# Linear attention block: the inverse deviation of the first four tiles computed on GpSimd, and one weight load moved ahead of one load of x

## The chip, the cores and the metric

The kernel runs on one core of a Trainium2 chip. Its time is the device time in microseconds (us) of one execution. Median before: 105.94 us over 3 runs (105.9 to 106.11).

A core has five engines that run their own instruction streams in order and meet through semaphores: TensorE (PE in the profile; its weight loads are PEld), VectorE (DVE), ScalarE (ACT), GpSimd (POOL) and SyncE (SP), which here only issues DMAs.

## The reference

Input x has 2048 rows of 640 columns, bf16. Three things are added up.

```python
x  = A_x
xn = (x - mean(x)) / sqrt(var(x) + 1e-5)          # per row
# A: linear attention with 32 heads of 20 columns
q, k, v = xn @ wqkv                                # 640 x 1920
phi(t) = where(t > 0, t + 1, exp(t)) + 1e-6
kv  = sum over rows of phi(k)^T v;  z = sum over rows of phi(k)
A   = (phi(q) kv / (phi(q) z + 1e-6)) @ wo
# B: the 8 rows with the largest x . w_r get a gated MLP, scaled by sigmoid(x . w_r)
out = x + A + (xn + MLP on its 8 rows)
```

B is applied to xn, so its row scores are xn times w_r, and its residual is xn. What the change touches is the first line: the mean and the inverse deviation of each row.

## The kernel before

The rows are worked in 16 tiles of 128 (`t` is the tile). Four stages follow each other: k for all tiles and the sum G = xn^T phi(k); q for all tiles; the small products of kv, wo and the MLP; and the output tiles. The change lies at the start of the first stage, in the code written out by hand for tiles 0 to 3. There is no scheduler: `ctx.enter_context(tc.manual_schedule())` is set, so each engine executes its instructions in the order in which the code issues them.

For one tile, the steps and their names are these.

- `ld(sp, XX[:, t, 1, :], ...)` (L103): SyncE issues the load of x. The loads of tiles 0 to 3, the second half of the k weights and the remaining tiles stand one after the other in SyncE's queue. The first half of the k weights goes through ScalarE's queue.
- `ln_a`, `ln_b` (L149, L152): VectorE takes the statistics of columns 0 to 319 and 320 to 639.
- `ln_g` (L155): VectorE makes mean and variance of them, in `MVf` (the aggregate).
- `ln_r` (L158, L159): ScalarE computes the inverse deviation `SR` as exp(-0.5 ln(var + eps)), two instructions on one column.
- `ln_xn` (L163): VectorE makes (x - mean) times SR. This is the normalization that the prediction speaks of. For tile 0 it comes in two parts, columns 0 to 255 and 256 to 639.
- `tr_mm` (L172): TensorE transposes the normalized tile into PSUM; `tr_cp` (L179 on ScalarE, L181 on VectorE) copies it to `xnT`.
- `K(t, (h,), ...)` (L208): TensorE multiplies with half h of the k weights, `wkh[h]`.
- `PHe`, `PHr`, `PHb` (L224, L227, L243): ScalarE takes exp and relu, VectorE combines them into `pk`, that is phi(k). `G` (L252, L259) sums over the rows.
- `ones(t)` (L265): GpSimd writes a column of ones into the normalized tile, for z.

From tile 4 on, the transposes are DMAs (L184) and the loop over t issues everything; `pool_extra` holds the building of constants that GpSimd does in the loop. `consts_e` and `bm2_copies` build a mask, `bm2`, that is first read where kv is masked, after the q stage.

Of the hand-written start, the part that matters reads as follows:

```python
    ln_a(0); ln_b(0); ln_a(1); ln_g(0); ln_b(1)
    ln_r(0)
    ln_g(1)
    ln_xn(0, ((0, 2 * P),))
    ln_r(1)
    ln_xn(0, ((2 * P, D),))
    ...
    ln_xn(1)
```

(The first line is five lines in the code.)

Of the kernel before, what the change touches and what calls it, by code (L numbers as in the profile page):

```python
# [7 lines left out]
P = 128  # L8
S = 2048
D = 640  # L10
# [13 lines left out]
EPS_BF16 = 1.0013580322265625e-05  # L24
# [6 lines left out]
F32 = mybir.dt.float32  # L31
# [3 lines left out]
ALU = mybir.AluOpType  # L35
# [3 lines left out]
def kernel(  # L39
# [13 lines left out]
    pe, dve, act, pool, sp = nc.tensor, nc.vector, nc.scalar, nc.gpsimd, nc.sync  # L53
# [3 lines left out]
    wqkv_v = A_wqkv.rearrange("(kc p) n -> p kc n", p=P)  # L57
# [9 lines left out]
    def st(shape, dt, name, tag=None):  # L67
        return sb.tile(shape, dt, name=name, tag=tag or name)
# [18 lines left out]
    lowkey = st([P, T], I32, "lowkey")  # L87
    eps6 = st([P, 1], F32, "eps6")
    eps5 = st([P, 1], F32, "eps5")
    lnv = st([P, T], F32, "lnv")  # L90
    rbf = st([P, T], BF16, "rbf")
    MVf = st([P, T, 2], F32, "MVf")
    MV = MVf[:].bitcast(BF16).rearrange("p t (k o) -> p t k o", o=2)[:, :, :, 1]
    SR = st([P, T], F32, "SR")
# [3 lines left out]
    HW = 320  # L98
    wkh = [wk[:, :, 0:HW], wk[:, :, HW + 64 :]]


    def ld(eng, dst, src):
        eng.dma_start(dst, src)  # L103
# [7 lines left out]
    ld(act, wkh[0], wqkv_v[:, :, D : D + HW])  # L111
    ld(sp, XX[:, 1, 1, :], x_v[:, 1, :])
    ld(sp, XX[:, 2, 1, :], x_v[:, 2, :])
    ld(sp, XX[:, 3, 1, :], x_v[:, 3, :])
    ld(sp, wkh[1][:, :, 0:HW], wqkv_v[:, :, D + HW : 2 * D])
    for a, b in ((4, 8), (8, 12), (12, 16)):
        ld(sp, XX[:, a:b, 1, :], x_v[:, a:b, :])
    sp.dma_start_transpose(xnT[:, 0:4, S - P : S], zero[:])
# [1 line left out]
    def warm4(w):  # L120
        pe.matmul(PS[:, 7, 0:w], lhsT=nc.const_aps.tensor(0.0, (P, P), F32),
                  rhs=nc.const_aps.tensor(0.0, (P, w), F32), start=True, stop=True)

    dve.memset(eps5[:], EPS_BF16)
    pool.memset(ident[:], 0.0)
    pool.affine_select(
        out=ident[:], in_=ident[:], compare_op=ALU.not_equal, fill=1.0,
# [19 lines left out]
    def ln_a(t):  # L147
        sts[t] = tmp.tile([P, 2, nc.vector.BN_STATS_DIM], F32, tag="stats", name="stats", bufs=4)
        dve.bn_stats(out=sts[t][:, 0, :], in_=XX[:, t, 1, 0:320])  # L149

    def ln_b(t):
        dve.bn_stats(out=sts[t][:, 1, :], in_=XX[:, t, 1, 320:D])  # L152

    def ln_g(t):
        dve.bn_aggr(out=MV[:, t, :], in_=sts[t][:])  # L155

    def ln_r(t):
        act.activation(lnv[:, t : t + 1], MV[:, t, 1:2], AF.Ln, bias=eps5[:])  # L158
        act.activation(SR[:, t : t + 1], lnv[:, t : t + 1], AF.Exp, scale=-0.5)  # L159

    def ln_xn(t, parts=((0, D),)):
        for a, b in parts:
            dve.tensor_scalar(out=XX[:, t, 0, a:b], in0=XX[:, t, 1, a:b], scalar1=MVf[:, t, 0:1],  # L163
                              scalar2=SR[:, t : t + 1], op0=ALU.subtract, op1=ALU.mult)
# [3 lines left out]
    def tr_mm(t, h, b0):  # L168
        k0, k1 = TRP[h]
        pt = PS[:, b0 + h, :].bitcast(BF16)  # L170
        for kc in range(k0, k1):
            pe.transpose(pt[:, (kc - k0) * P : (kc - k0 + 1) * P], XX[:, t, 0, kc * P : (kc + 1) * P], ident[:])  # L172

    def tr_cp(t, h, b0, eng):
        k0, k1 = TRP[h]
        src = PS[:, b0 + h, :].bitcast(BF16)[:, 0 : (k1 - k0) * P].rearrange("p (k c) -> p k c", c=P)
        dst = xnT[:, k0:k1, t * P : (t + 1) * P]
        if eng is act:
            act.copy(dst, src)  # L179
        else:  # L180
            dve.tensor_copy(dst, src)  # L181
# [17 lines left out]
    def off(t, h):  # L199
        return T - 1 - t if t != 1 and h else 0  # L200

    def K(t, hs=(0, 1), b=6, ks=range(KC)):
        for h in hs:
            if t > 4:
                pad(1)
            w = HW + h
            for kc in ks:
                pe.matmul(  # L208
                    PS[:, b + h, off(t, h) : off(t, h) + w],
                    lhsT=xnT[:, kc, t * P : (t + 1) * P],  # L210
                    rhs=wkh[h][:, kc, 0:w],
                    start=(kc == 0),
                    stop=(kc == KC - 1),
                )
# [6 lines left out]
    def PHe(t, h, b=6):  # L221
        if t not in phis:
            phis[t] = tuple(tmp.tile([P, D], BF16, tag=k, name=k, bufs=3) for k in ("ek", "rk"))
        act.activation(phis[t][0][:, h * HW : (h + 1) * HW], phi_src(t, h, b), AF.Exp)  # L224

    def PHr(t, h, b=6):
        act.activation(phis[t][1][:, h * HW : (h + 1) * HW], phi_src(t, h, b), AF.Relu)  # L227
# [17 lines left out]
    def pad(n):  # L245
        for _ in range(n):
            pe.ldweights(zero[:, 0:P])  # L247
# [30 lines left out]
    def band(ap, base, n, w=DH):  # L278
        for k, (b0, sg) in enumerate(((base, 1), (w - 1 - base, -1))):
            pool.affine_select(  # L280
                out=ap, in_=ap, compare_op=ALU.is_ge, fill=0.0,
                base=b0, pattern=[[-sg * w, n], [0, w]], channel_multiplier=sg,
            )

    def consts_e():
        pool.memset(bm2[0:E2, :], 1.0)
        band(bm2[0:E2, :], P, 8)

    def bm2_copies(gs):
        for g in gs:  # L290
            pool.tensor_copy(bm2[32 * g : 32 * g + 32, :], bm2[0:E2, :])
# [14 lines left out]
    def consts_d():  # L306
        pool.iota(lowkey[:], pattern=[[P, T]], base=P - 1, channel_multiplier=-1)

    pool_extra = {3: consts_b, 4: consts_c, 5: consts_d}

    wo_v = A_wo.rearrange("(g r) d -> r g d", r=GC)
    wg_v = B_w_gate.rearrange("(kc p) n -> p kc n", p=P)
# [19 lines left out]
                ld(sp, wg[:, k, :], wg_v[:, k, :])  # L332


    consts_e()
    bm2_copies((1, 2, 3))
    KA, KB = (range(0, 2), range(2, KC))
    ln_a(0)
    ln_b(0)
    ln_a(1)  # L340
    ln_g(0)
    ln_b(1)
    ln_r(0)
    ln_g(1)
    ln_xn(0, ((0, 2 * P),))
    ln_r(1)
    ln_xn(0, ((2 * P, D),))
    tr_mm(0, 0, 0)
    ln_xn(1)
# [5 lines left out]
    tr_cp(0, 1, 0, act)  # L355
    K(0, (0,), 6, KA)
    ln_b(2)
    tr_cp(1, 0, 2, act)
    tr_mm(1, 1, 2)
    ones(1)  # L360
    K(0, (0,), 6, KB)
    tr_cp(1, 1, 2, act)
    ln_g(2)
    ln_a(3)
    K(1, (0,), 4, KA)
    ln_r(2)
    ln_b(3)
    K(1, (0,), 4, KB)
    PHe(0, 0, 6)
    ln_xn(2)  # L370
    K(0, (1,), 6, KA)
    PHr(0, 0, 6)
    K(1, (1,), 4, KA)
    ln_g(3)
    ln_r(3)
    tr_mm(2, 0, 0)
    K(0, (1,), 6, KB)
    tr_cp(2, 0, 0, act)
# [113 lines left out]
    for t in range(T - 1):  # L492
# [13 lines left out]
                      op0=ALU.arith_shift_right, op1=ALU.bitwise_and)  # L506
# [445 lines left out]
```

## Time and profile before

| | us |
|---|---|
| median of 3 runs | 105.94 |
| the profiled execution | 105.91 |
| its span | 104.2 |
| TensorE busy | 99.8 (96%) |
| VectorE busy | 82.7 (79%) |
| ScalarE busy | 69.1 (66%) |
| GpSimd busy | 17.1 (16%) |

All times in the text are us from the start of the span. A row of the timeline or of the groups names the line, the engine, the operation, what it writes and reads with shapes, and how many. In the timeline the first number is the start and the second the length; a bracket at the end gives the idle time of the engine ahead of it and what ended it. Instructions of one engine overlap: the next one can start while the last one drains, so the distance between two starts is shorter than a length. In a DMA row the last number is the time from the issue to the landing. The granted TensorE clock was 1.00 in every stretch of the first 20 us of this run.

### The profile page before, as it was taken

To read this page: it belongs to the slowest core of one execution; us is meant where nothing else is said; L and a number is where in the kernel's file an instruction comes from. 1 tells how busy PE (TensorE), PEld (TensorE's weight loads), DVE (VectorE), ACT (ScalarE), POOL (GpSimd) and SP (SyncE) were. 2 spreads that over 40 slices of the span, in tenths; PEclk is the share of its full clock that TensorE was granted. 3 is DMA by queue.
4 is the path that set the end of the run, shared out by engine and by line. 5 is a ranking of instruction groups with operands and counts; after the bars stand their busy time and mean duration, and the time that the engine had idled before them with its cause. 6 is when DMAs were issued, how large, how long until landed. Compare 5 with 4: busy or idle time off the path is not lost.

```text
span 104.2 us, 2816 instructions
## 1 busy us (share of the span) xinstructions
PE 99.8 (96%) x944; PEld 72.5 (70%) x1176; DVE 82.7 (79%) x186; ACT 69.1 (66%) x174; POOL 17.1 (16%) x57
## 2 busy tenths in 40 slices
PE   6999999999999999999999999999999999999980
PEld 3347666668888888888877777875577667777760
DVE  1797999988888898873887886778988997888870
ACT  4289957666666666888599989997983997000000
POOL 7700000620000000000000064460001500000500
PEclk9999999999999999999999999999999999999999
DMA  2999937334557755889999999901760039983344
GB/s 63 298 307 377 325 66 69 66 66 92 135 127 92 140 124 124 191 248 359 224 399 249 360 406 382 319 22 31 217 236 9 12 110 270 280 289 122 126 129 126
DMA packets 23408, 19.77 MB, mean 190 GB/s; under 512 B 10978, under 2 KB 21858, under 8 KB 23394
## 3 DMA queue, kind: packets, MB, share of 16 engines
q1 hardware_dynamic: 22152, 19.11, 63.2%
q10 hardware_dynamic: 954, 0.46, 1.7%
q8 instruction: 8, 0.13, 0.6%
q0 software_dynamic: 288, 0.01, 0.3%
q14 instruction: 6, 0.05, 0.2%
HBM read 13.80 MB, written 3.65 MB: 168 GB/s over the span
## 4 chain that ended last, share of the span: by engine, by line
PE 89%; DVE 3%; DMA 2%; issue 2%; DVEq 0%
PE PS L208 21%; PE PS L480 21%; PE PS L751 20%; PE PS L252 16%; PE PS L259 4%; DMA XX<-in_A_x_dram 2%; PE PS L708 2%; PE PS L672 1%; PE PS L551 1%; PE PS L172 1%; PE PS L727 1%; PE PS L273 1%; DVE stats L149 1%; DVE XX L163 1%; DVE stats L152 1%
## 5 line engine op out<-in xcount | busy, mean ns | idle before, releaser
L208 PE MATMUL PS<-wk,xnT 128*128 128x320 bf16 (+1 forms) x160 | 25.2, 300 | 0.0
L252 PE MATMUL PS<-pk,XX 128*128 128x512 bf16 x75 | 22.7, 379 | 0.0
L247 PEld LDWEIGHTS <-zero 128*128 128x128 bf16 x224 | 18.2, 97 | 5.7
L480 PE MATMUL PS<-xnT,wq 128*128 128x512 bf16 x97 | 21.8, 379 | 0.3 <-issue 0.2
L751 PE MATMUL PS<-Mb,pqT 128*128 128x320 bf16 (+4 forms) x165 | 22.1, 295 | 0.0
L224 ACT ACTIVATE ek<-PS 128x320 bf16<-128x320 f32 x32 | 14.1, 441 | 9.9 <-PE PS L208 9.9
L751 PEld LDWEIGHTS <-pqT 128*128 128x128 bf16 x165 | 15.8, 98 | 4.5 <-issue 0.2
L208 PEld LDWEIGHTS <-xnT 128*128 128x128 bf16 x160 | 15.1, 97 | 4.5 <-ACT xnT L179 0.2
L243 DVE SCALAR_TENSOR_TENSOR pk<-ek,rk 128x640 bf16<-128x640 bf16 x16 | 13.1, 820 | 4.8 <-ACT rk L227 4.5
L542 DVE SCALAR_TENSOR_TENSOR pqT<-qe,qr 128x512 bf16<-128x512 bf16 x20 | 13.5, 682 | 2.5 <-ACT qr L489 2.5
L488 ACT ACTIVATE qe<-PS 128x512 bf16<-128x512 f32 x20 | 12.5, 624 | 2.9 <-PE PS L480 2.3
L259 PE MATMUL PS<-pk,XX 128*128 128x128 bf16 x64 | 14.0, 219 | 0.3
L227 ACT ACTIVATE rk<-PS 128x320 bf16<-128x320 f32 x32 | 14.0, 437 | 0.0
L480 PEld LDWEIGHTS <-wq 128*128 128x128 bf16 x100 | 11.6, 118 | 2.9
L489 ACT ACTIVATE qr<-PS 128x512 bf16<-128x512 f32 x20 | 12.5, 626 | 0.0
L760 DVE TENSOR_TENSOR o<-PS,XX 128x640 bf16<-128x640 f32 x11 | 9.0, 823 | 2.9 <-PE PS L751 1.4
L252 PEld LDWEIGHTS <-XX 128*128 128x128 bf16 x80 | 7.8, 98 | 4.5
L196 ACT ACTIVATE XX<-XX,MR,SR 128x640 bf16<-128x640 bf16 x11 | 9.4, 913 | 0.0
L149 DVE BATCH_NORM_STATS2 stats<-XX 128x6 f32<-128x320 bf16 x16 | 7.4, 461 | 2.0 <-DMA XX<-in_A_x_dram 2.0
L163 DVE TENSOR_SCALAR XX<-XX,MVf,SR 128x640 bf16<-128x640 bf16 (+2 forms) x17 | 7.2, 433 | 0.6 <-ACT SR L159 0.6
L152 DVE BATCH_NORM_STATS2 stats<-XX 128x6 f32<-128x320 bf16 x16 | 7.7, 482 | 0.0
L265 POOL MEMSET XX<- 128x1 bf16 x18 | 1.9, 107 | 35.4 <-DVE XX L163 15.5
(111 smaller groups left out, 102.1 us busy)
## 6 DMA issues: line engine op xcount, KB each, us to landing
out_dram<-o SPq DMA_DIRECT2D x15, 160.0 KB, 2.7
XX<-in_A_x_dram SPq DMA_DIRECT2D x3, 640.0 KB, 7.9
wg<-in_B_w_gate_dram SPq DMA_DIRECT2D x5, 384.0 KB, 7.7
wd<-in_B_w_down_dram SPq DMA_DIRECT2D x1, 1920.0 KB, 13.3
wu<-in_B_w_up_dram SPq DMA_DIRECT2D x1, 1152.0 KB, 6.3
wv<-in_A_wqkv_dram SPq DMA_DIRECT2D x5, 160.0 KB, 2.6
wq<-in_A_wqkv_dram SPq DMA_DIRECT2D x1, 800.0 KB
hi_d<-XX SPq DMA_DIRECT2D x1, 800.0 KB, 4.0
```

The costliest lines, as they stand in the source:

```text
L208: pe.matmul(PS[:, b + h, off(t, h) : off(t, h) + w], lhsT=xnT[:, kc, t * P : (t + 1) * P], rhs=wkh[h][:, kc, 0:w], start=(kc == 0), stop=( ...
L224: act.activation(phis[t][0][:, h * HW : (h + 1) * HW], phi_src(t, h, b), AF.Exp)
L227: act.activation(phis[t][1][:, h * HW : (h + 1) * HW], phi_src(t, h, b), AF.Relu)
L243: dve.scalar_tensor_tensor(out=pk[:, t, :], in0=ek[:], scalar=1.0, in1=rk[:], op0=ALU.min, op1=ALU.add)
L247: pe.ldweights(zero[:, 0:P])
L252: pe.matmul(PS[:, a, :], lhsT=lhsT, rhs=pk[:, t, 0:512], start=(t == 0), stop=(t == T - 1),)
L259: pe.matmul(PS[:, 5, a * P : (a + 1) * P], lhsT=lhsT, rhs=pk[:, t, 512:D], start=(t == 0 and a == 0), stop=(t == T - 1), skip_group_check= ...
L480: pe.matmul(PS[:, bank, :], lhsT=by5(wq[:, kc, :])[:, m, :], rhs=xnT[:, kc, tb * TBLK : (tb + 1) * TBLK], start=(kc == 0), stop=(kc == KC ...
L488: act.activation(e, PS[:, bank, :], AF.Exp)
L489: act.activation(r, PS[:, bank, :], AF.Relu)
L542: dve.scalar_tensor_tensor(out=pqT[:, m, tb * TBLK : (tb + 1) * TBLK], in0=e, scalar=1.0, in1=r, op0=ALU.min, op1=ALU.add,)
L751: pe.matmul(PS[:, b, o : o + c1 - c0], lhsT=pqT[:, kc, t * P : (t + 1) * P], rhs=Mb[:, kc, c0:c1], start=(kc == 0), stop=(kc == KC - 1))
```

## The change

For tiles 0 to 3, `ln_r` is replaced by `ln_p`: GpSimd adds eps to the variance and raises the sum to the power -0.5, taken from a column `mhalf`. Later tiles keep `ln_r`. The order of the issue is changed around it. Tile 0's first part of the normalization stands ahead of tile 1's aggregate; tile 3's statistics stand behind tile 2's normalization. The load of the second half of the k weights stands ahead of the load of x of tile 3. The building of `bm2` moves from the start into the loop, after tile 6.

```diff
+    mhalf = st([P, 1], F32, "mhalf")
...
+    ld(sp, wkh[1][:, :, 0:HW], wqkv_v[:, :, D + HW : 2 * D])
     ld(sp, XX[:, 3, 1, :], x_v[:, 3, :])
-    ld(sp, wkh[1][:, :, 0:HW], wqkv_v[:, :, D + HW : 2 * D])
...
+    dve.memset(mhalf[:], -0.5)
...
+    def ln_p(t):
+        pool.tensor_scalar(out=lnv[:, t : t + 1], in0=MV[:, t, 1:2], scalar1=EPS_BF16, scalar2=None, op0=ALU.add)
+        pool.tensor_tensor(out=SR[:, t : t + 1], in0=lnv[:, t : t + 1], in1=mhalf[:], op=ALU.pow)
...
+    def consts_f():
+        consts_e()
+        bm2_copies((1, 2, 3))
-    pool_extra = {3: consts_b, 4: consts_c, 5: consts_d}
+    pool_extra = {3: consts_b, 4: consts_c, 5: consts_d, 6: consts_f}
...
-    consts_e()
-    bm2_copies((1, 2, 3))
...
     ln_g(0)
+    ln_p(0)
     ln_b(1)
-    ln_r(0)
+    ln_xn(0, ((0, 2 * P),))
     ln_g(1)
-    ln_xn(0, ((0, 2 * P),))
-    ln_r(1)
+    ln_p(1)
     ln_xn(0, ((2 * P, D),))
...
     ln_b(2)
+    ln_g(2)
+    ln_p(2)
     tr_cp(1, 0, 2, act)
...
-    ln_g(2)
-    ln_a(3)
     K(1, (0,), 4, KA)
-    ln_r(2)
-    ln_b(3)
     K(1, (0,), 4, KB)
     PHe(0, 0, 6)
     ln_xn(2)
+    ln_a(3)
+    ln_b(3)
     K(0, (1,), 6, KA)
     PHr(0, 0, 6)
     K(1, (1,), 4, KA)
     ln_g(3)
-    ln_r(3)
+    ln_p(3)
```

VectorE's order, from tile 0's aggregate to tile 3's normalization, before (BN_STATS are the statistics, BN_AGGR the aggregate, TENSOR_SCALAR the normalization; from top to bottom tiles 0, 1, 2, 3):

```order
L155 BN_AGGR MVf<-stats 128x2
L152 BN_STATS stats<-XX 128x6
L155 BN_AGGR MVf<-stats 128x2
L163 TENSOR_SCALAR XX<-XX,MVf,SR 128x256
L163 TENSOR_SCALAR XX<-XX,MVf,SR 128x384
L163 TENSOR_SCALAR XX<-XX,MVf,SR 128x640
L149 BN_STATS stats<-XX 128x6
L152 BN_STATS stats<-XX 128x6
L155 BN_AGGR MVf<-stats 128x2
L149 BN_STATS stats<-XX 128x6
L152 BN_STATS stats<-XX 128x6
L163 TENSOR_SCALAR XX<-XX,MVf,SR 128x640
```

The same stretch of VectorE's order in the changed kernel (its line numbers are a few higher):

```order
L157 BN_AGGR MVf<-stats 128x2
L154 BN_STATS stats<-XX 128x6
L169 TENSOR_SCALAR XX<-XX,MVf,SR 128x256
L157 BN_AGGR MVf<-stats 128x2
L169 TENSOR_SCALAR XX<-XX,MVf,SR 128x384
L169 TENSOR_SCALAR XX<-XX,MVf,SR 128x640
L151 BN_STATS stats<-XX 128x6
L154 BN_STATS stats<-XX 128x6
L157 BN_AGGR MVf<-stats 128x2
L169 TENSOR_SCALAR XX<-XX,MVf,SR 128x640
L151 BN_STATS stats<-XX 128x6
L154 BN_STATS stats<-XX 128x6
```

Two things moved: tile 1's aggregate went behind the first part of tile 0's normalization, and tile 3's two statistics went behind tile 2's normalization. TensorE's order is the same in both kernels, row for row.

GpSimd's order in the changed kernel, from the last memset of the preamble on, for tiles 0 to 3 (MEMSET XX is `ones`):

```order
L145 MEMSET xsT 128x160
L164 TENSOR_SCALAR lnv<-MVf 128x1
L165 TENSOR_TENSOR SR<-lnv,mhalf 128x1
L164 TENSOR_SCALAR lnv<-MVf 128x1
L165 TENSOR_TENSOR SR<-lnv,mhalf 128x1
L271 MEMSET XX 128x1
L164 TENSOR_SCALAR lnv<-MVf 128x1
L165 TENSOR_TENSOR SR<-lnv,mhalf 128x1
L271 MEMSET XX 128x1
L164 TENSOR_SCALAR lnv<-MVf 128x1
L165 TENSOR_TENSOR SR<-lnv,mhalf 128x1
```

Before, the building of `bm2` stood between the first of these rows and the first `ones`, and there was no arithmetic on the tiles.

## The prediction

> **What bounds the kernel now.** I read the page's busy shares first, then the chain of work that ended last, then the waits of TensorE's weight loads, then the timeline of the first 10 us. The page:
>
> ```profile
> PE 99.8 (96%) x944; PEld 72.5 (70%) x1176; DVE 82.7 (79%) x186; ACT 69.1 (66%) x174; POOL 17.1 (16%) x57
> PE 89%; DVE 3%; DMA 2%; issue 2%; DVEq 0%
> ```
>
> A share of 96% says little by itself. The chain (start, length, what) says where the end is set:
>
> ```profile
> 5.54 0.80 DVE XX L163 x2
> ...
> 6.38 0.29 PE PS L172 x2
> ...
> 6.93 0.17 PE PS L172 x3
> ...
> 9.49 0.41 PE PS L208 x3
> ...
> 70.13 0.18 issue
> ```
>
> Until 6.38 us the chain runs through the first load of x and VectorE. From there it is TensorE alone, and the longest pause that it shows up to TensorE's last matmul is the 0.18 us at 70.13. So the time is the moment at which TensorE gets tile 1's normalized x, plus a fixed stream, plus any stall added to that stream. A microsecond put in early is not won back, since no later wait is long enough to swallow it. In the first 12 us TensorE's weight loads wait for two things:
>
> ```profile
> PEld L172 <- DVE XX L163: 2.0, 4, 1.4
> PEld L208 <- ACT xnT L179: 0.2, 1, 0.2
> ```
>
> These are the transposes (L172), which wait for the normalization on VectorE (L163), and once a copy on ScalarE. No k weights are in the list. Now the timeline of the four tiles:
>
> ```profile
> 4.48 0.20 DVE L155 BATCH_NORM_AGGREGATE MVf<-stats 128x2 bf16<-128x12 f32 x1
> 4.71 0.29 ACT L158 ACTIVATE lnv<-MVf,eps 128x1 f32<-128x1 bf16 x1 [0.63 <-DVE MVf L155]
> 5.04 0.20 ACT L159 ACTIVATE SR<-lnv 128x1 f32<-128x1 f32 x1
> 5.06 0.21 DVE L155 BATCH_NORM_AGGREGATE MVf<-stats 128x2 bf16<-128x12 f32 x1
> 5.27 0.34 DVE L163 TENSOR_SCALAR XX<-XX,MVf,SR 128x256 bf16<-128x256 bf16 x1
> 5.87 0.45 DVE L163 TENSOR_SCALAR XX<-XX,MVf,SR 128x640 bf16<-128x640 bf16 x1
> 6.23 0.49 DVE L149 BATCH_NORM_STATS2 stats<-XX 128x6 f32<-128x320 bf16 x1
> 6.64 0.48 DVE L152 BATCH_NORM_STATS2 stats<-XX 128x6 f32<-128x320 bf16 x1
> 7.15 0.21 DVE L155 BATCH_NORM_AGGREGATE MVf<-stats 128x2 bf16<-128x12 f32 x1
> 7.27 0.44 DVE L149 BATCH_NORM_STATS2 stats<-XX 128x6 f32<-128x320 bf16 x1
> 7.63 0.48 DVE L152 BATCH_NORM_STATS2 stats<-XX 128x6 f32<-128x320 bf16 x1
> 8.08 0.45 DVE L163 TENSOR_SCALAR XX<-XX,MVf,SR 128x640 bf16<-128x640 bf16 x1
> 8.58 0.16 PEld L172 LDWEIGHTS <-XX 128*128 128x128 bf16 x2
> 9.24 0.45 DVE L163 TENSOR_SCALAR XX<-XX,MVf,SR 128x640 bf16<-128x640 bf16 x1 [0.60 <-ACT SR L159]
> 9.74 0.11 PEld L172 LDWEIGHTS <-XX 128*128 128x128 bf16 x2 [0.18 <-DVE XX L163]
> ```
>
> Read it as four handovers from aggregate to normalization. Tile 0's aggregate ends at 4.68, and ScalarE's two functions let the normalization start at 5.27: 0.59 us. In that gap VectorE does the rest of tile 1's statistics. Tile 2's gap, 7.36 to 8.08, holds both statistics of tile 3. So ScalarE's latency is mostly covered by VectorE's own work. Tiles 2 and 3 are ready just in time: the normalizations end at 8.53 and 9.69, and the transposes' weight loads start at 8.58 and 9.74, each 0.05 later. TensorE is there no earlier: the matmuls ahead of tile 3's transposes run to 9.49 + 0.41 = 9.90 in the chain, so these start while those still drain.
>
> **The change, part by part.** *The power.* ScalarE's 0.29 + 0.20 go; GpSimd gets an add and a power on one column each. The trace has neither operation, so each is bounded by the nearest rows of GpSimd:
>
> ```profile
> 7.16 0.10 POOL L265 MEMSET XX<- 128x1 bf16 x1 [0.64 <-DVE stats L152]
> L265 POOL MEMSET XX<- 128x1 bf16 x18 | 1.9, 107 | 35.4 <-DVE XX L163 15.5 <-DMA xnT<-XX 12.9 <-DVE MVf L155 3.2
> L651 POOL COPY kv<-kv 32x40 bf16<-32x40 bf16 x4 | 0.8, 210 | 1.3 <-DVE kv L640 1.2
> L297 POOL TENSOR_SCALAR_AFFINE_SELECT bm<-bm 128x32 f32<-128x32 f32 x2 | 1.1, 568 | 0.1
> 69.01 0.76 POOL L651 COPY kv<-kv 64x40 bf16<-64x40 bf16 x1
> 69.01 0.69 DVE L542 SCALAR_TENSOR_TENSOR pqT<-qe,qr 128x512 bf16<-128x512 bf16 x1
> 60.81 1.47 POOL L608 COPY xsT<-xnT 128x5 bf16 x1 [16.22 <-DMA wu<-in_B_w_up_dram]
> ```
>
> The lower bound is the one-column MEMSET, 0.107 us, which writes as much and reads nothing; the upper bound that I use for the power is the mean AFFINE_SELECT, 0.57. I take the small COPY's 0.21 for both: it reads and writes as they do, and with few columns most of it is fixed cost. GpSimd reacts 0.06 after what it waits for (the MEMSET at 7.16, behind transposes that end at 7.10), and the power must wait for the add. VectorE reacts 0.03 after its releaser (5.24 to 5.27). One handover is H = 0.06 + 0.21 + 0.06 + 0.21 + 0.03 = 0.57 us, against 0.59 on ScalarE: no gain in itself. What decides is the order on VectorE.
>
> *Tile 0 and 1.* Tile 0's first part now runs ahead of tile 1's aggregate. It starts at 4.68 + 0.57 = 5.25 instead of 5.27. The aggregate follows 0.27 later (5.54 less 5.27), at 5.52, and ends at 5.73, where it was 5.27. A second whole handover comes behind it. Tile 0's second part then occupies VectorE from 5.64 (0.12 on, as 7.15 to 7.27) to 6.01 (0.37 for its 384 columns, between 0.34 for 256 and 0.45 for 640), and the add falls into that. The COPY at 69.01 shows the price: beside a VectorE instruction that ended at 69.70 it ended at 69.77, 0.07 later, instead of after 0.21. So the add ends at 6.08 instead of 6.00 (c = 0.08). The power ends at 6.35, and tile 1's normalization starts at 6.38 instead of 5.87: **+0.51 us** at the point where TensorE's stream begins.
>
> The Trainium skill, "SBUF — State Buffer", section "SBUF: two separate sides", states that VectorE and GpSimd share a port pair which one instruction holds to its end. Its section on the bandwidth-pool intuition puts the blocked side at about 115 ns past VectorE's end. If the add only begins to read then, it ends about 0.25 us later than by the row, and the estimate by that page is 107.4 us in all. The rows agree that one waits for the other; that a whole instruction still follows behind the wait they do not show.
>
> *Tile 2 and 3.* From a normalization to the next tile's first statistics is 0.36 (5.87 to 6.23), to the second 0.41, to the aggregate 0.51, to its end 0.21: 1.49. Tile 2 starts at 6.38 + 1.49 + 0.57 = 8.44 (before 8.08) and ends at 8.89; TensorE, itself 0.51 late, wants it at 9.09. That passes. But tile 3's statistics, which had filled tile 2's wait, now come behind tile 2's normalization, and VectorE idles through the 0.57. Tile 3 starts at 8.44 + 1.49 + 0.57 = 10.50 instead of 9.24: **+1.26 us**. TensorE would be there at 9.74 + 0.51 = 10.25 and waits until 11.00, 0.75 more. What is late next is only what follows it: TensorE keeps its order, and VectorE's and ScalarE's work behind tile 3 moves along.
>
> In general the shift is 4H + c - 1.10. Four handovers stand in series on 4.68 + 0.27 + 0.21 + 1.49 + 1.49 = 8.14, and before tile 3 started at 9.24, 1.10 later.
>
> *The loads.* SP's queue carries x of tile 3 and then the k weights' half:
>
> ```profile
> 2.20 0.43 SPq L103 DMA_DIRECT2D XX<-in_A_x_dram  x1
> XX<-in_A_x_dram SPq DMA_DIRECT2D x1, 160.0 KB, 4.7
> 2.68 0.43 SPq L103 DMA_DIRECT2D wk<-in_A_wqkv_dram  x1
> wk<-in_A_wqkv_dram SPq DMA_DIRECT2D x1, 400.0 KB, 5.4
> ```
>
> The weights land at 2.68 + 5.4 = 8.08, and no wait names them, so having them earlier is worth nothing now. With the order turned, x of tile 3 lands last of the two, by the same bytes at about 8.08 instead of 2.20 + 4.7 = 6.9. Its statistics want it at 8.80. Nothing added. If that cover went (statistics ready before 8.08) it would become the bound.
>
> *The rest.* One more MEMSET on VectorE falls into its wait for the first x: nothing. The mask's building moves from the program's start into the loop, where GpSimd is busy 16% of the span: nothing, covered by its idle time. ScalarE loses about 2 us of work early: nothing, TensorE waits for ScalarE only 0.2 us there, behind a copy.
>
> The profiled execution took 105.91 us with a span of 104.2; 1.7 lies around it. The median is 105.94, 0.03 higher. 105.91 + 1.26 = **107.17, say 107.2 us**.
>
> **The rivals.** *The same path, other prices.* Both at 0.107: H = 0.36, shift 4 x 0.36 - 1.10 = +0.34, 106.25. The power at 0.57: H = 0.93, +2.70, 108.6. These are the bounds of the forecast itself.
>
> *A short handover: faster.* Place: GpSimd between aggregate and normalization. Faster begins below H = 0.275, where 4H is 1.10 (0.125 us for the two operations together), and only if x of tile 3 lands before 8.08: from its landing to tile 3's normalization is 0.41 + 0.51 + 0.21 + H. At 0.03 each, H is 0.21 and the shift -0.26, 105.65, for which x must be there at 7.6. For it: a MEMSET's 0.107 may be mostly latency that overlaps in a row of them. Against it: the power waits for the add's end, so latency counts twice.
>
> *No change.* The same place at H near 0.275 to 0.29: 105.9. For it speaks that the single handover equals ScalarE's already; against it that both operations would have to be as short as the shortest write-only instruction, and shorter.
>
> *A slow power.* If the power is a long routine, say the longest COPY's 1.47 us, H is 1.83 and the shift 4 x 1.83 + 0.08 - 1.10 = +6.3: 112.2. Against it: nothing on GpSimd at one column shows more than a tenth of that; for it, no power is in the trace.
>
> **How the numbers follow.** The forecast has 0.63, the slow power 0.13, no change 0.11, the short handover 0.13. About 0.2% (0.2 us) is what a measurement of this kernel can tell from no change. So faster is 0.13, same 0.11, slower 0.63 + 0.13 = 0.76. The forecast's own range is 106.2 to 108.6. The range for 8 in 10 takes in no change and the short handover, 105.6 to 108.8, and leaves out the slow power.
>
> **What would show it.** Right: tile 1's normalization near 6.4 and tile 3's near 10.5; VectorE idle ahead of tiles 1, 2 and 3 for GpSimd; TensorE's transposes of tile 3 behind an idle time of about 0.7 us; the stream after 11 us as before. Wrong: add and power together under 0.13 us; x of tile 3 landing after 8.8, which would make the load the cause; or transposes of tile 3 without a wait, which would mean that I misread who is late there.

## The result, and the profile after

The changed kernel took **108.68 us** (median of 5 runs, 108.63 to 108.74), the kernel before 105.94 beside it: slower by 2.74 us, a ratio of 1.0256 with a 95% interval of 1.0242 to 1.0269. Forecast were 107.2 and +1.26. The direction was right and the time lies inside the range, but the loss is more than twice the forecast one.

The profiled execution took 108.67 us with a span of 107.0 (before 105.91 and 104.2). Its page, busy time of the engines and shares of the chain that ended last:

```profile
PE 101.1 (94%) x944; PEld 73.4 (69%) x1176; DVE 82.8 (77%) x187; ACT 67.7 (63%) x166; POOL 20.6 (19%) x65
PE 88%; DVE 3%; DMA 2%; issue 2%; POOL 2%; DVEq 0%; POOLq 0%
```

GpSimd is 3.5 us busier, and it has entered the chain. The chain in order of time (start, length, what) says where:

```profile
4.71 0.24 POOL lnv L164
...
5.03 0.58 POOL SR L165
...
5.64 0.35 DVE XX L169
...
6.20 0.23 POOL lnv L164
...
6.51 0.57 POOL SR L165
...
7.12 0.46 DVE XX L169
7.58 0.05 issue
7.62 0.28 PE PS L178 x2
```

Until 7.62 the chain is two whole handovers, each an add and a power. Before, TensorE took over at 6.38. The timeline of VectorE from tile 0's aggregate to tile 3's normalization, without the rows of the statistics (both orders listed ahead of the prediction stop short of tile 3's aggregate and normalization, which come next in each):

```profile
4.43 0.19 DVE L157 BATCH_NORM_AGGREGATE MVf<-stats 128x2 bf16<-128x12 f32 x1
5.64 0.35 DVE L169 TENSOR_SCALAR XX<-XX,MVf,SR 128x256 bf16<-128x256 bf16 x1 [0.66 <-POOL SR L165]
5.90 0.20 DVE L157 BATCH_NORM_AGGREGATE MVf<-stats 128x2 bf16<-128x12 f32 x1
6.02 0.33 DVE L169 TENSOR_SCALAR XX<-XX,MVf,SR 128x384 bf16<-128x384 bf16 x1
7.12 0.45 DVE L169 TENSOR_SCALAR XX<-XX,MVf,SR 128x640 bf16<-128x640 bf16 x1 [0.77 <-POOL XX L271]
8.39 0.21 DVE L157 BATCH_NORM_AGGREGATE MVf<-stats 128x2 bf16<-128x12 f32 x1
9.60 0.45 DVE L169 TENSOR_SCALAR XX<-XX,MVf,SR 128x640 bf16<-128x640 bf16 x1 [1.00 <-POOL XX L271]
10.88 0.21 DVE L157 BATCH_NORM_AGGREGATE MVf<-stats 128x2 bf16<-128x12 f32 x1
12.08 0.45 DVE L169 TENSOR_SCALAR XX<-XX,MVf,SR 128x640 bf16<-128x640 bf16 x1 [1.00 <-POOL SR L165]
```

Read the gap between the end of each aggregate and the start of its normalization: 4.62 to 5.64, 6.10 to 7.12, 8.60 to 9.60, 11.09 to 12.08. Four handovers of 1.02, 1.02, 1.00 and 0.99 us, 4.03 in all, one after the other. (The brackets that name `XX L271` give the memset of ones that GpSimd runs right behind the power; the normalization needs the power.) The forecast had 0.57 for each. GpSimd's timeline, its adds and powers for tiles 1 and 2, shows what fills them:

```profile
6.20 0.23 POOL L164 TENSOR_SCALAR lnv<-MVf 128x1 f32<-128x1 bf16 x1 [0.59 <-DVE MVf L157]
6.51 0.57 POOL L165 TENSOR_TENSOR SR<-lnv,mhalf 128x1 f32<-128x1 f32 x1
8.69 0.22 POOL L164 TENSOR_SCALAR lnv<-MVf 128x1 f32<-128x1 bf16 x1 [1.56 <-DVE MVf L157]
9.00 0.57 POOL L165 TENSOR_TENSOR SR<-lnv,mhalf 128x1 f32<-128x1 f32 x1
```

The add takes 0.23, the power **0.57**. For tile 2: reaction to the aggregate 0.09 (8.60 to 8.69), add 0.22, 0.09 to the power, power 0.57, 0.03 to the normalization: 1.00.

What TensorE makes of it stands in its own timeline, first in this execution, then in one of a second profile of the changed kernel, which took 108.65:

```profile
7.62 0.28 PE L178 MATMUL PS<-ident,XX 128*128 128x128 bf16 x2 [0.88 <-DVE XX L169]
...
8.18 3.36 PE L214 MATMUL PS<-wk,xnT 128*128 128x320 bf16 x12
...
12.59 0.29 PE L178 MATMUL PS<-ident,XX 128*128 128x128 bf16 x2
```

```profile
8.14 1.86 PE L214 MATMUL PS<-wk,xnT 128*128 128x320 bf16 x12
...
12.54 0.29 PE L178 MATMUL PS<-ident,XX 128*128 128x128 bf16 x2 [1.21 <-DVE XX L169]
```

The kernel before had, for the same transposes:

```profile
9.75 0.28 PE L172 MATMUL PS<-ident,XX 128*128 128x128 bf16 x2
```

They start at 12.59 instead of 9.75: 2.84 later, and 9.24 to 12.08 is the same 2.84 for the normalization ahead of them. From there nothing is won back: the span is 107.0 - 104.2 = 2.8 longer. In the second profile TensorE stands idle for 1.21 us ahead of these transposes. In the first one it does not, since its twelve k matmuls ran at half their rate (3.36 against 1.86 us), which filled the same gap. The time is the same either way, and what that half rate is worth is taken up with the experiments.

### The profile page after: what moved, and what is told of

Same layout as the page of the kernel before. It is cut to its first block, busy times and chain, and to the rows that moved or that the text cites. A ratio compares the mean times of both kernels' runs of the same rounds, so it can differ in the third digit from the quotient of the medians.

```text
span 107.0 us, 2817 instructions
## 1 busy us (share of the span) xinstructions
PE 101.1 (94%) x944; PEld 73.4 (69%) x1176; DVE 82.8 (77%) x187; ACT 67.7 (63%) x166; POOL 20.6 (19%) x65
## 4 chain that ended last, share of the span: by engine, by line
PE 88%; DVE 3%; DMA 2%; issue 2%; POOL 2%; DVEq 0%; POOLq 0%
PE PS L214 22%; PE PS L488 20%; PE PS L759 19%; PE PS L258 15%; PE PS L265 4%; DMA XX<-in_A_x_dram 2%; PE PS L716 2%; PE PS L680 1%; POOL SR L165 1%; PE PS L178 1%; PE PS L559 1%; PE PS L735 1%; PE PS L279 1%; DVE stats L151 1%; DVE XX L169 1%
## 5 line engine op out<-in xcount | busy, mean ns | idle before, releaser
L214 PE MATMUL PS<-wk,xnT 128*128 128x320 bf16 (+1 forms) x160 | 26.8, 312 | 0.0
L214 PEld LDWEIGHTS <-xnT 128*128 128x128 bf16 x160 | 15.9, 101 | 5.1
L488 PEld LDWEIGHTS <-wq 128*128 128x128 bf16 x100 | 11.6, 118 | 2.9
L271 POOL MEMSET XX<- 128x1 bf16 x18 | 2.0, 113 | 29.1 <-DMA xnT<-XX 16.9
```

The costliest lines, as they stand in the source:

```text
L214: pe.matmul(PS[:, b + h, off(t, h) : off(t, h) + w], lhsT=xnT[:, kc, t * P : (t + 1) * P], rhs=wkh[h][:, kc, 0:w], start=(kc == 0), stop=( ...
L488: pe.matmul(PS[:, bank, :], lhsT=by5(wq[:, kc, :])[:, m, :], rhs=xnT[:, kc, tb * TBLK : (tb + 1) * TBLK], start=(kc == 0), stop=(kc == KC ...
```

## The experiments

The theory after the result: four handovers in series on VectorE, each 1.0 us, of which the power is the piece that was sized too small. The first rival is that the order costs nothing and GpSimd's operations do all of it; the second that TensorE's halved rate, not VectorE's chain, sets the end. Times are medians. The kernel before, run beside each, had medians from 105.96 to 106.44, so a difference of less than half a microsecond between lines far apart says little; the ratios are to the runs beside.

| kernel | us | ratio to before (95%) |
|---|---|---|
| the change, again | 108.70 | 1.0236 (1.0182 to 1.029) |
| order and loads alone, ScalarE's functions | 107.18 | 1.0113 (1.0082 to 1.0144) |
| the same again | 107.53 | 1.0121 (1.0075 to 1.0166) |
| ScalarE's functions at the power's places | 107.17 | 1.0114 (1.0083 to 1.0145) |
| GpSimd's operations alone, order before | 107.24 | 1.0101 (1.0042 to 1.016) |
| multiply for power | 107.12 | 1.01 (1.0076 to 1.0124) |
| the change, tile 3's statistics back | 107.71 | 1.0172 (1.0125 to 1.0219) |
| GpSimd for tiles 0 and 1 only (TensorE's rate full in one run of four) | 108.59 | 1.0147 (1.0039 to 1.0255) |
| the same, TensorE kept busy | 107.81 | 1.0134 (1.0065 to 1.0204) |
| the change, TensorE kept busy | 109.87 | 1.0326 (1.0259 to 1.0393) |
| the same again | 109.23 | 1.0285 (1.023 to 1.0339) |
| before, loads turned | 106.60 | 1.005 (1.0024 to 1.0075) |

### The order without the power

```diff
-    ln_p(0)      # and 1, 2, 3
+    ln_r(0)      # tile 2's behind K(1, (0,), 4, KA)
```

> The changed kernel with its order, its loads and its moved mask, but with ScalarE's logarithm and exponential for tiles 0 to 3 again (for tiles 2 and 3 at the places in ScalarE's order that they had before). Theory A, four handovers in series on VectorE: the shift is 4H - 1.10 with ScalarE's H of 0.59 to 0.65, so +1.3 to +1.5, 107.2 to 107.4 us, with tile 3's normalization starting near 10.5. Theory B, the power alone is at fault and the order is harmless: within 0.2 of 105.9. Theory C, the halved TensorE clock between 8.2 and 11.6 us sets the time: TensorE waits about 0.5 less long here, the clock stays full, and only the late start is left, 106.4.

Measured: 107.18 (9 runs, 107.08 to 108.27), +1.2. So the order costs by itself what the forecast gave the whole change, and the power is not the whole cause. That is no accident: with ScalarE one handover is 0.59, and the forecast had put GpSimd's at 0.57. Its repetition:

> The kernel of e1_order_only once more, since the profiled execution there ran with TensorE's clock not yet full until 10.4 us (108.27, where the other eight were mostly 107.1 to 107.3). Theory A: 107.1 to 107.4, and in a profile with the clock full tile 3's normalization between 10.4 and 10.7.

Measured: 107.53 over 4 runs, 107.07 to 108.02, a little above what was expected. Its two runs at the full mean clock took 107.26 and 107.07. In this kernel tile 2's logarithm stands behind two copies in ScalarE's queue, and these wait for TensorE. Both profiled executions were the longest of their runs (108.27 and 108.02), and in both TensorE was slow: its twelve k matmuls took 3.04 and 2.90 us, where they take 1.86 at full rate.

```profile
7.83 3.04 PE L214 MATMUL PS<-wk,xnT 128*128 128x320 bf16 x12
```

So the copies came late there, and tile 2 was normalized late behind them (at 9.02 and 9.31). No trace shows this kernel in one of its usual runs of about 107.1. To see whether the 1.2 us belong to the series of handovers or to ScalarE's queue, ScalarE's pair was put at the places of the add and the power:

```diff
     ln_b(2)
     ln_g(2)
-    ln_p(2)
+    ln_r(2)      # and tiles 0, 1, 3 in the same way
     tr_cp(1, 0, 2, act)
```

> The changed kernel with ScalarE's logarithm and exponential at exactly the places where the add and the power stand (in the order-alone kernel tile 2's pair stood behind two copies in ScalarE's queue, and tile 2 started at 9.02). Theory A (four handovers in series on 8.05 us, whichever engine makes them): with 0.59 a handover tile 1 starts near 6.3, tile 2 near 8.3 to 8.4, tile 3 near 10.4, 8.05 + 4 x 0.59, so about 1.2 later than before and 107.1 us, as the order-alone kernel's full-clock runs; the rest up to 108.7 is the price of the power alone, 4 x 0.4. Theory B (the order-alone kernel lost its 1.2 us to ScalarE's queue, not to the series): with the pair ahead of the copies the loss goes, 106.2 or less. Theory C (the pair now holds up tile 1's copies, which wait behind it for tile 2's aggregate until about 8.4): TensorE waits for those copies, the time is above 107.6.

Measured: 107.17 (6 runs, 107.08 to 108.1). VectorE's timeline:

```profile
4.74 0.20 DVE L157 BATCH_NORM_AGGREGATE MVf<-stats 128x2 bf16<-128x12 f32 x1
...
8.68 0.45 DVE L169 TENSOR_SCALAR XX<-XX,MVf,SR 128x640 bf16<-128x640 bf16 x1 [0.60 <-ACT SR L161]
9.96 0.21 DVE L157 BATCH_NORM_AGGREGATE MVf<-stats 128x2 bf16<-128x12 f32 x1
10.77 0.45 DVE L169 TENSOR_SCALAR XX<-XX,MVf,SR 128x640 bf16<-128x640 bf16 x1 [0.60 <-ACT SR L161]
```

From tile 0's aggregate (end 4.94) to tile 3's normalization it is 5.83 us; in the changed kernel, same order and same places, 7.46 (4.62 to 12.08). The difference, 1.63 for four handovers of 0.60 instead of 1.01, is the price of GpSimd against ScalarE, and the runs show 108.68 - 107.17 = 1.51. Tile 0's aggregate ended 0.32 later in this execution; without that tile 3 would start at 10.45, 1.21 later than before, near the median's loss of 1.12 against the runs beside it. TensorE was slow in this execution too (the last section has the row), and came to tile 3's transposes only at 12.00:

```profile
12.00 0.27 PE L178 MATMUL PS<-ident,XX 128*128 128x128 bf16 x2
```

So the trace shows the series on VectorE, and not the end that a usual run has. With the copies out of the pair's way the median is the same (107.17 and 107.18): the order's 1.2 us belong to the series of handovers, and ScalarE's queue does not show in them.

### The operations without the order

```diff
     ln_g(0)
     ln_b(1)
-    ln_r(0)
+    ln_p(0)      # and 1, 2, 3, each at ln_r's place; loads as before
```

> The kernel before, in its order and with its loads, with GpSimd's add and power in place of ScalarE's two functions for tiles 0 to 3 (and the mask built later, so that GpSimd is free). Theory A: with the statistics of the next tile inside the wait, only part of the four handovers (about 1.0 us each) stands in series: tile 1's normalization at 6.55, tile 2's at 9.0, tile 3's at 10.6 instead of 9.24, so +1.3, 107.3 us. Theory B, the power alone: as slow as the changed kernel, 108.7. Theory C: start 0.7 late, and 1.5 more if the clock halves: 106.6 or 108.1.

Measured: 107.24 (4 runs, 107.11 to 107.6). VectorE's timeline, tiles 1, 2 and 3:

```profile
6.59 0.45 DVE L169 TENSOR_SCALAR XX<-XX,MVf,SR 128x640 bf16<-128x640 bf16 x1 [0.23 <-POOL SR L165]
...
9.07 0.45 DVE L169 TENSOR_SCALAR XX<-XX,MVf,SR 128x640 bf16<-128x640 bf16 x1 [0.25 <-POOL SR L165]
...
10.64 0.45 DVE L169 TENSOR_SCALAR XX<-XX,MVf,SR 128x640 bf16<-128x640 bf16 x1 [1.00 <-POOL XX L271]
```

In the old order the handover of 1.0 is still partly covered: VectorE waits 0.23 and 0.25 where it waits 0.77 and 1.00 in the changed kernel, and only tile 3 pays in full. Against the runs beside them the order alone costs 1.22 us and the operations alone 1.28; together that is 2.50, most of the whole 2.74. (The mask's building stays moved in both.)

### The power's own price

```diff
-    ...tensor_tensor(out=SR..., in0=lnv..., in1=mhalf[:], op=ALU.pow)
+    ...tensor_tensor(out=SR..., in0=lnv..., in1=mhalf[:], op=ALU.mult)
```

> The changed kernel with GpSimd's second operation a multiply instead of a power (it leaves out the power, so the normalization is another number). It prices the power against a two-input operation on one column. Theory A: if the multiply takes about as long as the add, 0.23, each handover is 0.34 shorter and the time 4 x 0.34 = 1.36 less than the changed kernel's, 107.3 us. If the 0.57 is what any two-input operation takes there, 108.7. Theory C (clock): in between only if the clock still halves.

Measured: 107.12 (11 runs, 107.05 to 107.64). GpSimd's timeline, tile 0:

```profile
4.72 0.23 POOL L164 TENSOR_SCALAR lnv<-MVf 128x1 f32<-128x1 bf16 x1 [1.88 <-DVE MVf L157]
5.03 0.19 POOL L165 TENSOR_TENSOR SR<-lnv,mhalf 128x1 f32<-128x1 f32 x1
```

The same instruction on the same column with a multiply takes 0.19, with the power 0.57. The power itself is 0.38 us of the handover, four times 0.38 is 1.52, and the runs differ by 108.68 - 107.12 = 1.56. So the 0.21 that the forecast took from a small copy was right for an add and for a multiply, and wrong for a power. (In the profiled execution of this kernel, 107.64, x of tile 2 landed late, and VectorE idled 0.41 us for it; its later starts are not used here.)

### Tile 3's statistics back ahead of tile 2's normalization

```diff
+    ln_a(3)
     K(1, (0,), 4, KA)
+    ln_b(3)
     K(1, (0,), 4, KB)
     PHe(0, 0, 6)
     ln_xn(2)
-    ln_a(3)
-    ln_b(3)
```

> The changed kernel with tile 3's statistics ahead of tile 2's normalization again, inside its wait; tile 1's aggregate stays behind tile 0's first part, and GpSimd does all four powers. Theory A: tile 1's normalization at 7.1 and tile 2's at 9.6 as in the changed kernel, tile 3's at 9.6 + 0.36 + 0.21 + 1.0 = 11.2 instead of 12.1, 0.9 less: 107.8 us, where TensorE's clock stays full. Where it halves between 8 and 11.6 us, TensorE itself is not there before 12.6 and the time is 108.6, as in e6_tiles01.

Measured: 107.71 (4 runs, 107.68 to 108.4). VectorE's timeline, tile 3:

```profile
11.15 0.45 DVE L169 TENSOR_SCALAR XX<-XX,MVf,SR 128x640 bf16<-128x640 bf16 x1 [1.00 <-POOL XX L271]
```

Tile 3 starts at 11.15 instead of 12.08, and the time falls by 1.0. One of the four handovers is again filled with the next tile's statistics. This isolates the step of the forecast by which VectorE idles ahead of tile 2 instead of doing tile 3's statistics.

### Is it TensorE's rate?

In the first profile TensorE ran at half rate from 8.2 to 11.6, so that it reached tile 3's transposes just when they were ready. To tell the causes apart, two matmuls of zeros were put into TensorE's idle stretches:

```diff
+    warm4(256)
     tr_mm(0, 0, 0)
...
     tr_mm(0, 1, 0)
+    warm4(512)
```

> The changed kernel with two more idle-time matmuls of zeros on TensorE, one ahead of tile 0's transposes and one between tile 0's and tile 1's, where TensorE waits anyway; nothing else is changed. The clock should stay at 1.0 throughout. Theory A (tile 3's normalization at 12.1 us sets the time): the same as the changed kernel, 108.7, with an idle time of some 1.3 us ahead of tile 3's transposes. Theory C (the halved clock sets it): 1.4 to 1.6 us faster than the changed kernel, about 107.2.

Measured: 109.87 (4 runs), not less. TensorE's timeline:

```profile
12.61 0.28 PE L178 MATMUL PS<-ident,XX 128*128 128x128 bf16 x2 [1.22 <-DVE XX L169]
```

At full rate there it idles 1.22 us and starts tile 3's transposes at 12.61, as in the changed kernel. So the rate is not what sets the end there; VectorE's chain is. The repetition of the changed kernel says the same without an edit:

> The changed kernel itself, on the same chip as e5b_warm, e6_tiles01 and e7_tiles01_warm: 108.7, with a clock that halves in some executions (8.2 to 11.6 us) and not in others, at the same time.

Measured: 108.70, with 108.65, 108.75 and 108.65 at a mean clock of 1.0 and 108.80 at 0.984.

Why the kernel with the matmuls of zeros lost another microsecond was looked for with a repetition:

> The kernel of e5_warm once more, beside the changed kernel itself on the same chip. In e5_warm tile 3's transposes started at 12.61 us, as in the changed kernel (12.58), with a full clock; the stream then waited 1.5 us at 52.6 for the load of the q weights, which landed at 54.15 instead of 51.27. Theory A: without that late landing 108.7, the same as the changed kernel. If the late landing comes with the added matmuls, again 109.3 or more.

Measured: 109.23. TensorE's waits in it hold one that the changed kernel has not (engine, line, what it waited for, us in total, times, longest):

```profile
PEld L214 <- DMA xnT<-XX: 0.4, 1, 0.4
```

In all three profiles with added matmuls the first DMA transpose, of tile 4, landed 3.5 to 4.2 us after its issue, where it took 2.6 to 2.7 in the eleven other profiles. In the first of them TensorE also waited 1.5 us for the q weights. Why these transfers are slower with two more matmuls was not found.

Next, GpSimd for tiles 0 and 1 only, tiles 2 and 3 as before, which takes tile 3's lateness away:

```diff
-    ln_g(2)
-    ln_p(2)
     tr_cp(1, 0, 2, act)
...
+    ln_g(2)
+    ln_a(3)
     K(1, (0,), 4, KA)
+    ln_r(2)
+    ln_b(3)
     K(1, (0,), 4, KB)
```

> The changed kernel with GpSimd's power for tiles 0 and 1 alone; tiles 2 and 3 have ScalarE's functions and their statistics in the order before. Tile 1's normalization should start near 7.1 as in the changed kernel (1.25 late), tile 3's near 10.4, before TensorE wants it. Theory A (VectorE's chain): what is left is the late start, +1.25, 107.2 us, if TensorE's clock stays full. Theory C (the idle TensorE before 7.6 us halves its clock for 3.4 us, which costs up to 1.6): about 108.7, as slow as the changed kernel, wherever the clock does halve.

Measured: 107.02 at a mean clock of 1.0, and 108.55, 108.62 and 108.68 at 0.983 to 0.984. Here the rate counts. TensorE's timeline, in the execution at 108.62:

```profile
7.69 0.74 PE L214 MATMUL PS<-wk,xnT 128*128 128x320 bf16 x2
8.22 0.53 PE L178 MATMUL PS<-ident,XX 128*128 128x128 bf16 x3
8.54 3.01 PE L214 MATMUL PS<-wk,xnT 128*128 128x320 bf16 x12
...
12.49 0.28 PE L178 MATMUL PS<-ident,XX 128*128 128x128 bf16 x2
```

Tile 3 was normalized by 11.34, but TensorE only came at 12.49, without a wait: its two, three and twelve instructions had taken 0.31, 0.20 and 1.15 us more than at full rate (0.43, 0.33, 1.86), 1.66 together. The other three runs are 1.53 to 1.66 longer than 107.02. With the matmuls of zeros added:

> The kernel of e6_tiles01 with the two matmuls of zeros in TensorE's idle times, so that its clock stays full. Both theories: +1.25, 107.2 us. The difference to e6_tiles01 is the price of the halved clock where nothing else hides it: 0 by theory A if the clock doesn't matter there, up to 1.6 by theory C.

Measured: 107.87, 107.57 and 107.74, and one run of 112.56 whose clock was 0.983 and which nothing here explains. In the profiled execution the loss was 1.16 us at tile 3's transposes (10.91 instead of 9.75), near the 1.25 expected for two tiles, and 1.92 at tile 4's first k matmul (18.59 instead of 16.67), which waits for the late DMA transpose. The median of the three runs, 107.74, is 0.88 below that of the three half-rate runs without the matmuls of zeros; with the 0.76 of the late transfer that is the 1.6 again.

### The loads alone

```diff
+    ld(sp, wkh[1][:, :, 0:HW], wqkv_v[:, :, D + HW : 2 * D])
     ld(sp, XX[:, 3, 1, :], x_v[:, 3, :])
-    ld(sp, wkh[1][:, :, 0:HW], wqkv_v[:, :, D + HW : 2 * D])
```

> The kernel before with nothing changed but SP's queue: the second half of the k weights ahead of x of tile 3. The weights should land near 7.5 instead of 8.05, x of tile 3 near 7.9 instead of 6.9. Tile 3's statistics, which start at 7.27 before, would then wait until 7.9 and push tile 2's normalization, behind them on VectorE, from 8.08 to about 8.7: TensorE wants tile 2 at 8.58 with a normalization begun at 8.08, so +0.6 if nothing gives way, 106.5 us. If the load order is free, as the prediction put it: within 0.2 of 105.9.

Measured: 106.60 (12 runs, 106.28 to 107.22), 0.5% slower. VectorE's timeline:

```profile
8.03 0.49 DVE L149 BATCH_NORM_STATS2 stats<-XX 128x6 f32<-128x320 bf16 x1 [0.39 <-DMA XX<-in_A_x_dram]
8.44 0.48 DVE L152 BATCH_NORM_STATS2 stats<-XX 128x6 f32<-128x320 bf16 x1
8.83 0.43 DVE L163 TENSOR_SCALAR XX<-XX,MVf,SR 128x640 bf16<-128x640 bf16 x1
```

In the old order tile 3's statistics stand ahead of tile 2's normalization, and x of tile 3 lands at 8.00. VectorE waits 0.39 us for it, and tile 2, which is ready, waits behind. In the changed order the statistics come at 9.96, and x, there at 7.90, is long landed. So the turned loads cost time with the statistics in their old place, and none that shows with the turned statistics: the two parts belong together.

No kernel here beats the one before. ScalarE's handover is shorter than GpSimd's, and the order before hides most of it.

## Why the prediction was right and wrong

**What bounds the kernel: right.** An early microsecond is not won back: 2.84 at tile 3's transposes, 2.8 at the end of the span.

**The series of four handovers: right.** With the measured handovers the formula's form holds: the four take 4.03, the rest of the way from the end of tile 0's aggregate to tile 3's normalization 12.08 - 4.62 - 4.03 = 3.43 (forecast 0.27 + 0.21 + 1.49 + 1.49 = 3.46). Undoing one of the series (tile 3's statistics back) gave back 1.0, one handover, and shortening each by 0.41 (ScalarE at the same places) gave back 1.5.

**The power at 0.21: wrong, and this is the step that failed.** "I take the small COPY's 0.21 for both: it reads and writes as they do, and with few columns most of it is fixed cost." That held for the add (0.23) and for a multiply (0.19). A power carries 0.38 more than the multiply on the same column, so most of it is not fixed cost. Of the 0.44 that each handover is longer, the power has 0.36, the two reactions of 0.09 instead of 0.06 have 0.06, and the add 0.02. The handover is 1.01 instead of 0.57, and the four of them 4.03 instead of 4 x 0.57 = 2.28, 1.75 more. The rest goes the other way: 0.08 for the shared port, which did not show, and 0.09 from the first aggregate's end (4.62 for 4.68) and the shorter rest of the way (3.43 for 3.46). 1.75 - 0.08 - 0.09 = 1.58; tile 3 was forecast for 10.50 and started at 12.08, just that much later. The upper bound that the text named, the AFFINE_SELECT's 0.57, happened to be the power's duration, and the sum with it gave 108.6. That it came so near was luck twice: another operation's duration was the same, and 0.31 too little for reactions and adds stood against 0.17 too much elsewhere. Between 0.107 and 0.57 a value was chosen by shape (columns read and written), where the kind of arithmetic decided.

**The port at 0.08: not seen on the add, but the wait exists.** On tile 1 the add ran from 6.20 to 6.43, most of it beside VectorE's second part of tile 0 (6.02 to 6.35), and took 0.23, where it took 0.22 on tile 2 with VectorE idle. It ended 0.08 after VectorE's instruction, so a wait for that instruction would fit into its own duration: it cost 0.01 at most, and these rows cannot tell whether there was one. The estimate by the page, by which the add would only begin to read behind VectorE's end, did not come true. The wait does show on GpSimd's memsets of one column. Each of these began beside a normalization of 640 columns on VectorE, in the kernel before, in the changed one and in the one with the operations alone:

```profile
9.55 0.18 POOL L265 MEMSET XX<- 128x1 bf16 x1 [2.29 <-PE PS L172]
12.40 0.17 POOL L271 MEMSET XX<- 128x1 bf16 x1 [0.35 <-PE PS L178]
6.82 0.25 POOL L271 MEMSET XX<- 128x1 bf16 x1 [0.27 <-PE PS L178]
```

The normalizations ended at 9.69, 12.53 and 7.04, the memsets at 9.73, 12.57 and 7.07: 0.17 to 0.25 us instead of 0.10, always up to 0.03 or 0.04 behind VectorE's end. Beside statistics a memset was not stretched (6.42 in the kernel before: 0.10 beside those from 6.23 to 6.72). The Trainium skill, "SBUF — State Buffer", section "SBUF: two separate sides", states that VectorE, in some of its instructions, and GpSimd exclude each other on the shared pair of ports, and that whichever starts first keeps it for its whole instruction. These memsets agree. (At 22.72 in the changed kernel one took 0.10 beside such a normalization, and it was VectorE's row that took 0.54 instead of 0.45.) The first of the three stands in the trace before and was there to be read; it also answers the prediction's "nothing on GpSimd at one column shows more than a tenth of that", since a tenth of 1.47 is 0.15.

**TensorE's idle 0.75 ahead of tile 3: right in place, 1.21 in size** in the execution at full rate. What was not foreseen is that TensorE can run at half rate after its waits ahead of tiles 0 and 1. In the changed kernel that is covered by the wait for tile 3; with tile 3 on time it cost 1.6 us. Whether those waits bring it about stays open: with the same waits the mean clock was 0.983 or 0.984 in 6 of 17 runs, with matmuls of zeros in them in 1 of 12, too few to tell.

**The loads: right for the changed kernel, incomplete.** x of tile 3 landed at 7.90 (forecast about 8.08), its statistics came at 9.96, and no wait names it. The text had said that if that cover went it would become the bound; the loads alone show that case, and 0.5% (0.2% to 0.8%) is what it costs without the turned statistics. The mask, the extra memset and ScalarE's relief were put at nothing, and nothing in the profile speaks against that; no run takes them alone.

**The rivals.** A short handover and no change both needed a handover of 0.29 or less; measured were 1.01. The slow power at 1.47 us was too slow by 0.9, though its reason, that no power was in the trace, was the right doubt.

## What to carry to other kernels

When an operation that the trace has never shown enters a series, its price counts as often as it stands there, so the distance between its bounds must be multiplied before one of them is chosen: here 0.36 us between two prices for the power were 1.44 us of time. A handover costs only what the waiting engine's other ready work does not cover: before moving such work, count how many of the handovers it was covering. And a load order and the place of its first reader in a queue are one decision: the turned loads alone cost time here.

## What the runs showed of the hardware

A power on GpSimd over one column of 128 partitions took 0.57 us, a multiply of the same operands 0.19, an add of a constant 0.23. GpSimd began 0.09 us after VectorE's aggregate ended and again 0.09 after its own preceding instruction. A memset of one column beside VectorE's normalization of 640 columns ended 0.03 to 0.04 us after it, in eight of the profiles; beside nothing of the kind it took 0.10.

TensorE fell to half rate in some executions of one kernel and not in others. In the first profile of the change the twelve k matmuls took 3.36 us, in the second 1.86. The windows of the first one show the granted clock in the column before the last two (after the busy shares of the five engines):

```profile
8.00:9.00 1.00, 1.00 (x9) 0.63 (x7) 0.57 (x2) 0.79 (x2) 0.22 (x2) 0.61 1.06 387
9.00:10.00 1.00, 1.00 (x5) 0.53 (x4) 0.40 (x2) 0.77 (x2) 0.61 (x2) 0.50 1.06 367
10.00:11.00 1.00, 1.00 (x5) 0.60 (x4) 0.96 (x4) 0.00 (x0) 0.00 (x0) 0.50 1.06 369
11.00:12.00 1.00, 1.00 (x8) 0.70 (x6) 0.09 (x1) 0.20 (x1) 0.74 (x2) 0.68 1.07 358
```

With the clock at 0.5 while it is low, the missing parts of these four rows (0.39, 0.50, 0.50, 0.32) are 1.71, so it was low for 3.4 us. The Trainium skill, "TensorE: Matmul & The Clock Gate", section "What's actually happening", has the array at half rate after at least one idle window of about 3.4 us, and the windows run freely. The length and the change from run to run agree with this trace. An idle stretch of that length did not come ahead of the fall here: TensorE idled for 0.64 and for 0.88 us, with five transposes of 0.70 us between. How little work makes a window count as idle, these runs do not show.

The record of the clock is also not always complete. In the profiled execution of the kernel with ScalarE's functions at the power's places, the same twelve matmuls took 2.93 us while the windows give a clock of 1.00:

```profile
8.14 2.93 PE L214 MATMUL PS<-wk,xnT 128*128 128x320 bf16 x12
```

That execution took 108.1, its median was 107.17. So a mean clock near 1.00 does not by itself show that TensorE ran at full rate; the durations of its matmuls do.
